# RWKV recurrence in chunks of 64 on four 64x64 array tiles, its output transposed and packed by DMA

## The chip, the cores and the metric

The kernel runs on one core of a Trainium2 chip. A core has a matrix engine (TensorE; PE in the profile, its weight loads PEld), three elementwise engines (VectorE, ScalarE, GpSimd; DVE, ACT, POOL) and a queue engine (SyncE, SP) that here issues every DMA. Each engine works through its own instruction list in order and waits on semaphores for the others. The metric is the device time of one execution, in microseconds (us), as the median of several runs.

## The reference

A recurrence (RWKV-6) over 4 batches, 8 heads, 768 time steps and 48 channels per head, followed by a two-layer MLP on the result, 3072 tokens of 384 channels:

```
for t in range(S):                       # per batch and head
    cur   = outer(u * k_t, v_t)          # [48, 48]
    y_t   = r_t @ (state + cur)
    state = w_t[:, None] * state + outer(k_t, v_t)
x = y.transpose(0, 2, 1, 3).reshape(3072, 384)
h = x @ w_in                             # [384, 2048]
out = gelu_exact(h) @ w_out              # [2048, 384]
```

The two weight matrices arrive as float64 and are turned into float32 on the chip.

## The kernel before

**The recurrence.** Two heads side by side fill the 128 partitions, 64 each (48 channels and zeros). The 768 steps of a head pair are 6 chunks of 128. Inside a chunk every pair (s, t) with s < t belongs to one of seven levels, h = 1 to 64. At each level one matrix product per chunk (`d`, line 191) gives all products of k (stationary, 128 columns) with the right halves of r (moving, 64 steps for each of two heads), and a masked copy out of PSUM (line 196, VectorE; for the last level a plain copy on ScalarE, line 194) keeps those of the level in `a`. Then r and k are multiplied by the other half's decay (line 205 on VectorE, a call for each head's 64 partitions; line 206 on GpSimd), and the halves' products `tots` are formed (line 208). The next level's `d` needs both. The diagonal (s = t) is a product apart: r times k on GpSimd (line 171), a matrix product with u (`dg_ps`, line 175), and `dv` on GpSimd (line 180). r lies in blocks with zeros for the other head, which is why one k serves both heads.

After the levels: transposes of k (`kt_ps`, line 218), each chunk's k v^T (`kv_ps`, line 223, the only products on part of the array: two 64-column halves), the states in front of the chunks one after the other (line 229, VectorE), and y (lines 236 and 238: `a` or r is stationary with 128 columns, v or the state moves with 48). y is in time-major order, so line 252 transposes x on TensorE into `xT` for the MLP.

**The MLP.** For 384 tokens at a time: 16 blocks of 3 products `h_ps` (line 262) and a GELU on ScalarE (line 265), then 3 blocks of 16 products `o_ps` (line 271), a copy (line 276) and the output's DMA.

**The order of the work.** Python generators set it. `attention` yields after each level; two head pairs go side by side, and after each yield some steps of the MLP of the batch before are put in. A scheduler then places the instructions on the engines by its own estimates. For the first batch the steps put in are instead the conversion of the weights: 28 pieces, each with a DMA, one ScalarE, five VectorE (lines 132 to 141) and one GpSimd instruction. The MLP of batch 0 therefore begins with the recurrence of batch 1, and the MLP of the last batch stands alone at the end. PSUM's 8 banks: 2 for `d`, 3 for the MLP, 2 for `misc`, 1 for y.

All data are float32. Each float32 product of the program is two weight loads and two matrix instructions in the trace (transposes are one), so the counts of the trace are twice the program's.

Of the kernel before, what the change touches and what calls it, by code (L numbers as in the profile page):

```python
# [20 lines left out]
DC = 3           # chunks of which a PSUM bank takes a level's products  # L21
PIECE = 512      # float64s of a row converted at once
# [7 lines left out]
def kernel(  # L30
    ctx: ExitStack,
    tc: tile.TileContext,
    rkw: bass.AP,      # [batch * head pair, 128, 3, time]: r, k, w, channels on partitions
    v: bass.AP,        # [batch * head pair, 128, 2, chunk, channel]: time on partitions
    u: bass.AP,        # [128, head pair, 2]: a head's u in its rows and its column, zeros elsewhere
# [15 lines left out]
    NU, _, _, S = rkw.shape  # L51
    D = v.shape[-1]
    NP = u.shape[1]
    B = NU // NP
    NC = S // C
    HC = C // 2
    N_TOK, DM = out.shape
    NJ = DM // 128
    DF = w_in.shape[1]
    NF = DF // 128  # L60
    TB = S // 2
    NT = TB // 128
# [9 lines left out]
    # r of a pair's heads in blocks, [head, channel] x [head, time]: zeros in the other two.  # L72
    r_bufs = [const.tile([128, 2, S], F32, name=f"r{i}") for i in range(4)]
    for r in r_bufs:
        nc.gpsimd.memset(r[0:G, 1, :], 0.0)
        nc.gpsimd.memset(r[G:, 0, :], 0.0)

    loaded = {}

    def load(n):  # L80
        if n >= NU:
            return
        r = r_bufs[n % len(r_bufs)]
        for g in range(2):
            nc.sync.dma_start(out=r[g * G:(g + 1) * G, g, :], in_=rkw[n, g * G:(g + 1) * G, 0, :])
        kw = io.tile([128, 2, S], F32, name="kw_in")
        nc.sync.dma_start(out=kw, in_=rkw[n, :, 1:3, :])
        x = io.tile([128, 2, NC, D], F32, name="v_in")
        nc.sync.dma_start(out=x, in_=v[n])
        loaded[n] = r, kw, x  # L90

    load(0)
    load(1)
    u_sb = const.tile([128, NP, 2], F32, name="u_sb")
    nc.sync.dma_start(out=u_sb, in_=u)

# [3 lines left out]
    # masks[h][s, (q, j)]: whether s is in the left half of the block q of 2h steps.  # L100
    masks = {}
    for h in LEVELS[:-1]:
        m = wk.tile([128, HC], F32, name="maskf")
        mv = m.rearrange("p (q j) -> p q j", j=h)
        nc.gpsimd.memset(m, 1.0)
        nc.gpsimd.affine_select(out=mv, in_=mv, compare_op=ALU.is_ge, fill=0.0, base=0,
                                pattern=[[-2 * h, HC // h], [0, h]], channel_multiplier=1)
        nc.gpsimd.affine_select(out=mv, in_=mv, compare_op=ALU.is_ge, fill=0.0, base=h - 1,
                                pattern=[[2 * h, HC // h], [0, h]], channel_multiplier=-1)
        masks[h] = const.tile([128, 1, HC], U8, name=f"mask{h}")  # L110
# [3 lines left out]
    a_bufs = [const.tile([128, NC, 2, C], F32, name=f"a{i}") for i in range(2)]  # L114
    for a in a_bufs:
        nc.vector.memset(a, 0.0)
# [4 lines left out]
    def to_float32(dst, src):  # L121
        """dst = src, float64s of which src's int64s hold the bits, rounded to float32."""
        n = src.shape[1]
        raw = cv.tile([128, PIECE], I64, name="raw")[:, 0:n]
# [5 lines left out]
        # What float32 has no exponent for: to 0, or to the largest.  # L130
# [5 lines left out]
        # The sign, the exponent and the mantissa's first 20 bits.  # L136
        nc.vector.scalar_tensor_tensor(out=f, in0=hi, scalar=0xC0000000, in1=f,  # L137
                                       op0=ALU.bitwise_and, op1=ALU.bitwise_or)
        # The other 32, as a number below the 20th; the sum rounds.
# [4 lines left out]

    def weights():
        pieces = [(w_in_sb[:, j, i:i + PIECE], w_in[j * 128:(j + 1) * 128, i:i + PIECE])
                  for i in range(0, DF, PIECE) for j in range(NJ)]
        pieces += [(w_out_sb[:, f, :], w_out[f * 128:(f + 1) * 128, :]) for f in range(NF)]
        for dst, src in pieces:
            if wide:  # L150
# [7 lines left out]
    def attention(n):  # L158
# [5 lines left out]
        if b not in x_of:  # L164
            x_of[b] = wk.tile([128, NC, DM], F32, name="x", bufs=1)
# [176 lines left out]
```

## Time and profile before

| | |
|---|---|
| median of 3 runs | 967.09 us (963.03 to 967.88) |
| profiled execution, span | 961.1 us |
| PE busy, weight loads busy | 860.9 us (90%), 623.9 us (65%) |
| VectorE, GpSimd, ScalarE busy | 447.7, 243.3, 123.3 us |
| instructions in the profile | 10766, of which 4248 matrix instructions |
| DMA | 41.59 MB, mean 43 GB/s |

The profiled execution's own time is its span, 961.1 us; the runs' median is 6 us above it. A row of the groups reads: line, engine, operation, tiles written and read, shape, count, then busy time and the mean length of one instruction. Mean lengths of matrix instructions contain the pipeline's depth, so the distance between starts says more: a merged row of the timeline or of the chain gives a count and the time they took together. PEclk is the share of TensorE's clock that was granted in a stage.

### The profile page before, as it was taken

To read this page: it belongs to the slowest core of one execution; us is meant where nothing else is said; L and a number is where in the kernel's file an instruction comes from. 1 tells how busy PE (TensorE), PEld (TensorE's weight loads), DVE (VectorE), ACT (ScalarE), POOL (GpSimd) and SP (SyncE) were. 2 spreads that over 40 slices of the span, in tenths; PEclk is the share of its full clock that TensorE was granted. 3 is DMA by queue.
4 is the path that set the end of the run, shared out by engine and by line. 5 is a ranking of instruction groups with operands and counts; after the bars stand their busy time and mean duration, and the time that the engine had idled before them with its cause. 6 is when DMAs were issued, how large, how long until landed. Compare 5 with 4: busy or idle time off the path is not lost.

```text
span 961.1 us, 10766 instructions
## 1 busy us (share of the span) xinstructions
PE 860.9 (90%) x4248; PEld 623.9 (65%) x4248; DVE 447.7 (47%) x812; ACT 123.3 (13%) x262; POOL 243.3 (25%) x236
## 2 busy tenths in 40 slices
PE   3748654889998999989998999989998999999998
PEld 3638653766766776766766676857676766655554
DVE  6898799875542553245533554155333543000000
ACT  0012010221110111011100111111100111120110
POOL 8645634334102411052204220052103210000000
PEclk9876556679999999989998999989998999999999
DMA  9033322420022001200031002200000000000000
GB/s 286 5 109 140 110 82 83 131 75 1 1 83 67 1 0 45 96 8 1 1 98 51 1 1 83 66 1 1 9 9 9 1 1 17 9 0 17 9 0 25
DMA packets 14850, 41.59 MB, mean 43 GB/s; under 512 B 2000, under 2 KB 5072, under 8 KB 14800
## 3 DMA queue, kind: packets, MB, share of 16 engines
q1 hardware_dynamic: 14800, 40.91, 13.2%
q8 instruction: 34, 0.56, 0.2%
q14 instruction: 16, 0.13, 0.0%
HBM read 36.18 MB, written 4.72 MB: 43 GB/s over the span
## 4 chain that ended last, share of the span: by engine, by line
PE 60%; issue 24%; DVE 11%; POOL 4%; DMA 1%; SPq 0%; ACT 0%; POOLq 0%
PE h_ps L262 26%; PE o_ps L271 14%; PE d L191 13%; DVE r L205 3%; DVE a L196 2%; PE dg_ps L175 2%; PE y L236 2%; POOL rk L171 2%; PE y L238 2%; DVE f L137 1%; DVE f L132 1%; DVE e L141 1%; DVE e L140 1%; DMA r<-in_rkw_dram 1%; POOL kw_in L206 1%
## 5 line engine op out<-in xcount | busy, mean ns | idle before, releaser
L262 PE MATMUL h_ps<-xT,w_in_sb 128*128 128x384 f32 x768 | 269.6, 503 | 0.0
L191 PE MATMUL d<-r,kw_in 128*128 128x128 f32 (+1 forms) x1344 | 207.9, 311 | 64.1 <-DVE a L196 54.6
L271 PE MATMUL o_ps<-w_out_sb,gt 128*128 128x384 f32 x768 | 260.8, 490 | 0.0
L191 PEld LDWEIGHTS d<-r,kw_in 128*128 128x128 f32 (+1 forms) x1344 | 193.0, 212 | 92.7 <-issue 49.7
L262 PEld LDWEIGHTS h_ps<-xT,w_in_sb 128*128 128x128 f32 x768 | 146.9, 198 | 90.7 <-issue 10.1
L196 DVE COPY_PREDICATED a<-mask,d 128x384 f32<-128x384 uint8 x192 | 131.8, 724 | 156.4 <-PE d L191 152.3
L271 PEld LDWEIGHTS o_ps<-w_out_sb,gt 128*128 128x128 f32 x768 | 141.2, 190 | 87.2 <-issue 1.0
L206 POOL TENSOR_TENSOR kw_in<-kw_in,tots 128x384 f32<-128x384 f32 x96 | 92.7, 966 | 289.7 <-PE d L191 281.1
L205 DVE TENSOR_TENSOR r<-r,tots 64x384 f32<-64x384 f32 x192 | 128.8, 671 | 44.0 <-PE d L191 40.9
L171 POOL TENSOR_TENSOR rk<-r,kw_in 64x768 f32<-64x768 f32 x32 | 60.3, 1885 | 203.3 <-PE dg_ps L175 201.2
L265 ACT ACTIVATE gt<-h_ps 128x384 f32<-128x384 f32 x128 | 62.7, 490 | 295.8 <-PE h_ps L262 295.8
L276 DVE COPY o_sb<-o_ps 128x384 f32<-128x384 f32 x24 | 13.4, 558 | 163.7 <-PE o_ps L271 163.7
L236 PE MATMUL y<-v_in,a 128*128 128x48 f32 x384 | 77.1, 300 | 1.1 <-DVE x L241 1.1
L236 PEld LDWEIGHTS y<-v_in,a 128*128 128x128 f32 x384 | 63.9, 216 | 12.1 <-DVE x L241 9.8
L238 PE MATMUL y<-state,r 128*128 128x48 f32 x320 | 68.0, 297 | 1.0 <-DVE state L229 0.6
L175 PE MATMUL dg_ps<-u_sb,rk 128*128 128x2 f32 x192 | 31.6, 292 | 28.0 <-POOL rk L171 24.6
L238 PEld LDWEIGHTS y<-state,r 128*128 128x128 f32 x320 | 54.6, 214 | 1.6 <-DVE state L229 1.0
L241 DVE TENSOR_TENSOR x<-y,dv 128x288 f32<-128x288 f32 x32 | 14.6, 457 | 86.8 <-PE y L238 86.8
L175 PEld LDWEIGHTS dg_ps<-u_sb,rk 128*128 128x128 f32 x192 | 31.3, 250 | 32.4 <-POOL rk L171 27.8
L205 DVE TENSOR_TENSOR r<-r,kw_in 64x384 f32<-64x384 f32 x32 | 39.5, 1233 | 2.4 <-POOL rk L171 1.9
L131 ACT ACTIVATE f<-raw 128x384 f32<-128x384 f32 (+1 forms) x28 | 16.9, 605 | 121.2 <-DMA raw<-in_w_out_dram 65.5
L208 DVE TENSOR_TENSOR tots<-tots 128x192 f32<-128x192 f32 (+5 forms) x96 | 30.4, 323 | 1.4
(37 smaller groups left out, 325.5 us busy)
## 6 DMA issues: line engine op xcount, KB each, us to landing
kw_in<-in_rkw_dram SPq DMA_DIRECT2D x16, 768.0 KB, 4.3
r<-in_rkw_dram SPq DMA_DIRECT2D x32, 192.0 KB, 3.2
raw<-in_w_in_dram SPq DMA_DIRECT2D x12, 512.0 KB, 3.6
raw<-in_w_out_dram SPq DMA_DIRECT2D x16, 384.0 KB, 3.0
v_in<-in_v_dram SPq DMA_DIRECT2D x16, 288.0 KB, 3.5
out_dram<-o_sb SPq DMA_DIRECT2D x24, 192.0 KB, 1.9
u_sb<-in_u_dram SPq DMA_DIRECT2D x1, 4.0 KB, 9.6
```

Source lines behind the costliest of these rows:

```text
L171: nc.gpsimd.tensor_mul(rk[half[g]], r[half[g], g], k[half[g]])
L175: nc.tensor.matmul(dg_ps[:, c, :], lhsT=rk[:, c * C:(c + 1) * C], rhs=u_sb[:, p, :], start=True, stop=True)
L191: nc.tensor.matmul(d[0:m, c - c0], lhsT=k[:, c * C:c * C + m], rhs=right[:, :, c], start=True, stop=True)
L196: nc.vector.copy_predicated(out=to[:, c0:c0 + DC].rearrange("p c g q j -> p (c g) q j"), mask=masks[h].rearrange("p o (q j) -> p o q j", j ...
L205: nc.vector.tensor_mul(r2, r2, t2[half[g], :, 0:1].to_broadcast([G, nb, h]))
L206: nc.gpsimd.tensor_mul(k2, k2, t2[:, :, 1:2].to_broadcast([128, nb, h]))
L208: nc.vector.tensor_mul(new, t2[:, :, 0], t2[:, :, 1])
L236: nc.tensor.matmul(y[:, c, :], lhsT=at[:, c, g, :], rhs=vt[:, g, c, :], start=True, stop=(c == 0))
L238: nc.tensor.matmul(y[:, c, :], lhsT=r[:, g, c * C:(c + 1) * C], rhs=state[:, c - 1, :], start=False, stop=True)
L262: nc.tensor.matmul(h_ps, lhsT=w_in_sb[:, j, f * 128:(f + 1) * 128], rhs=xT[:, j, :], start=(j == 0), stop=(j == NJ - 1))
L265: nc.scalar.activation(out=gt, in_=h_ps, func=AF.Gelu)
L271: nc.tensor.matmul(o_ps, lhsT=gs[f][:, i * 128:(i + 1) * 128], rhs=w_out_sb[:, f, :], start=(f == 0), stop=(f == NF - 1))
```

## The change

The chunks are 64 steps long instead of 128, so that k (64 partitions of a head, 64 steps) and `a` (64 by 64) fit a quarter of the array. There are now six levels, h = 1 to 32, and the work goes in tiles of 384 tokens: a tile has all 8 heads in two units of four heads (two head pairs, on the free axis). Eight tiles, 16 units.

- `products` (line 194) makes 24 products of 64x64 per level and unit; partition half g of the operands and half p of the output choose one of four array tiles, and the loop visits all four in turn. r is no longer laid out in blocks with zeros.
- The diagonal becomes a seventh set of such products, of k with r times u (`ru`, ScalarE, line 190), masked by the identity (line 204). `rk`, `dg` and `dv` are gone.
- Line 227 multiplies r for both heads in one call of 128 partitions.
- kv and y are 64x64 products too. y is computed transposed (v or the state stationary, `a` or r moving; lines 268 and 284), with all of a unit in two PSUM banks; the state's products wait for the first y products through a small VectorE copy (`fence`). States carry from one tile to the next of a batch.
- ScalarE copies y to `ysb`, and DMAs on SP's queue (line 295) put each head's 48 rows at its place in `xT`, in 10 pieces per tile. TensorE's transposes of x are gone.
- The main loop: during tile x's recurrence the MLP of tile x - 1 is put in, a step or more after each yield. The w_in pieces are converted in tile 0, the w_out pieces in tile 1 beside the MLP of tile 0. The four last steps or so of an MLP come after the recurrence's last yield.
- PSUM: 3 buffers of 2 banks for everything of the recurrence, 2 banks for the MLP.

How the instructions of TensorE stand in the middle of a batch, a level of two head pairs (r_73, r_74) and the next, before:

```order
L262 MATMUL h_ps<-xT,w_in_sb 128x384 x8
L191 MATMUL d<-r_73,kw_in 128x128 x6
L262 MATMUL h_ps<-xT,w_in_sb 128x384
L191 MATMUL d<-r_74,kw_in 128x128 x6
L262 MATMUL h_ps<-xT,w_in_sb 128x384 x8
```

And in the change, the diagonal and the first levels of a tile, both units (24 products each) in one row:

```order
L199 MATMUL d<-ru,rkw_in 64x64 x48
L311 MATMUL h_ps<-xT,w_in_sb 128x384 x9
L199 MATMUL d<-rkw_in 64x32 x48
L311 MATMUL h_ps<-xT,w_in_sb 128x384 x6
L199 MATMUL d<-rkw_in 64x32 x48
```

A level is now 48 small products instead of 12 large ones, with 6 products of the MLP behind it (9 before).

The end of a pair's recurrence and the beginning of the next on TensorE, before (v, a and the state make y; rk is GpSimd's r times k):

```order
L238 MATMUL y<-state,r_74 128x48
L271 MATMUL o_ps<-w_out_sb,gt 128x384 x9
L175 MATMUL dg_ps<-u_sb,rk 128x2 x6
L191 MATMUL d<-r_75,kw_in 128x128 x6
L262 MATMUL h_ps<-xT,w_in_sb 128x384
```

The same place in the change (st_147 and st_145 hold states):

```order
L284 MATMUL y_ps<-rkw_in,st_147 64x64
L284 MATMUL y_ps<-rkw_in,st_145 64x64 x8
L320 MATMUL o_ps<-w_out_sb,gt 128x384 x24
L199 MATMUL d<-ru,rkw_in 64x64 x48
L311 MATMUL h_ps<-xT,w_in_sb 128x384 x9
```

The 24 products of the MLP's end stand between the last y products of a tile and the first `h_ps` of the next, which read the packed `xT`.

VectorE in tile 1 of the change, where the conversion of w_out (lines 148 to 157) shares it with the levels (a_140 and a_141 are the two units' `a`):

```order
L220 COPY_PREDICATED a_140<-mask_122,d 128x48x8
L153 SCALAR_TENSOR_TENSOR f<-raw,f 128x384
L227 TENSOR_TENSOR rkw_in<-rkw_in,tots 128x48x8
L156 TENSOR_SCALAR e<-f 128x384
L148 TENSOR_SCALAR f<-f 128x384
L157 SCALAR_TENSOR_TENSOR e<-raw,e 128x384
L150 TENSOR_SCALAR f<-f 128x384
L220 COPY_PREDICATED a_141<-mask_122,d 128x48x8
```

In before all 28 pieces stood so among the levels of the first batch, with no product of the MLP beside them.

The diff, cut to its core:

```diff
-C = 128          # time steps of a chunk
-LEVELS = (1, 2, 4, 8, 16, 32, 64)
+C = 64
+T = 384
+Q = 2
+NC = T // C
+N3 = NC // 2
+NI = Q * N3
+LEVELS = (1, 2, 4, 8, 16, 32)
+BANK = 512
...
-    def attention(n):
+    def attention(n):
+        x, un = divmod(n, UB)
+        first = x % HALVES == 0
...
+        ru = wk.tile([128, Q * T], F32, name="ru")
+        for q in range(Q):
+            nc.scalar.activation(out=ru[:, q * T:(q + 1) * T], in_=r[:, q * T:(q + 1) * T], func=AF.Copy,
+                                 scale=u_sb[:, un * Q + q:un * Q + q + 1])
+        ruc = ru.rearrange("p (i c t) -> p i c t", c=2, t=C)
+
+        def products(right, width):
+            d = ps.tile([128, 2, BANK], F32, name="d", tag="d", bufs=3)
+            for i in range(NI):
+                for g in range(2):
+                    for p in range(2):
+                        nc.tensor.matmul(d[half[p], g, i * width:(i + 1) * width],
+                                         lhsT=kc[half[g], i, p], rhs=right(half[g], i, p), start=True, stop=True)
+            return d[:, :, 0:NI * width]
+
+        d = products(lambda z, i, p: ruc[z, i, p], C)
+        nc.vector.copy_predicated(out=at.rearrange("p g i t -> p (g i) t"),
+                                  mask=masks[0].to_broadcast([128, 2 * NI, C]), data=d)
+        yield
...
-            for g in range(2):
-                r2 = r[half[g], g].rearrange("p (n two j) -> p n two j", two=2, j=h)[:, :, 1, :]
-                nc.vector.tensor_mul(r2, r2, t2[half[g], :, 0:1].to_broadcast([G, nb, h]))
+            nc.vector.tensor_mul(r2, r2, t2[:, :, 0:1].to_broadcast([128, nb, h]))
...
+        for i in range(NI):
+            for p in range(2):
+                for g in range(2):
+                    nc.tensor.matmul(kv_ps[half[g], p, i * D:(i + 1) * D], lhsT=kt[half[p], i, g, :],
+                                     rhs=vc[i][g][half[p], 0:D], start=True, stop=True)
...
+        y_ps = ps.tile([128, 2, BANK], F32, name="y_ps", tag="d", bufs=3)
+        for i in range(NI):
+            for p in range(2):
+                for g in range(2):
+                    nc.tensor.matmul(y_ps[half[g], p, i * C:(i + 1) * C], lhsT=vc[i][g][half[p]],
+                                     rhs=at[half[p], g, i, :], start=(i == 0), stop=True, skip_group_check=True)
+        fence = wk.tile([128, 2], F32, name="fence")
+        nc.vector.tensor_copy(out=fence, in_=y_ps[:, :, NI * C - 1])
+        yield
+        for i in range(NI):
+            q, c3 = divmod(i, N3)
+            for p in range(2):
+                for g in range(2):
+                    c = 2 * c3 + (p + g) % 2
+                    src, c0 = (st, c - 1) if c else (before, NC - 1)
+                    if src is None:
+                        continue
+                    o = (q * NC + c0) * D
+                    nc.tensor.matmul(y_ps[half[g], c % 2, i * C:(i + 1) * C], lhsT=src[half[g], o:o + G],
+                                     rhs=rc[half[g], i, c % 2], start=False, stop=True, skip_group_check=True)
+        ysb = wk.tile([128, Q * T], F32, name="ysb")
+        nc.scalar.copy(out=ysb.rearrange("p (i c t) -> p c i t", c=2, t=C),
+                       in_=y_ps[:, :, 0:NI * C].rearrange("p c (i t) -> p c i t", t=C))
+        for q in range(Q):
+            for g in range(2):
...
+                    nc.sync.dma_start(out=xT[f0 % 128:f0 % 128 + f1 - f0, f0 // 128, :],
+                                      in_=ysb[e:e + f1 - f0, q * T:(q + 1) * T])
...
+        load(n + 2 * UB)
+        yield
...
+    for x in range(NX):
+        slots = zip(*(attention(x * UB + i) for i in range(UB)))
+        if x == 0:
+            spread(slots, weights(in_pieces), len(in_pieces), len(in_pieces))
+        else:
+            steps = mlp(x - 1)
+            if x == 1:
+                more = weights(out_pieces)
+                def both(a=steps, b=more):
+                    for _ in a:
+                        next(b, None)
+                        yield
+                steps = both()
+            n = NF + NT * NF // 4
+            spread(slots, steps, n, n - 4)
+    for _ in mlp(NX - 1):
+        pass
```

More of the change, by code (lines that the diff above doesn't have):

```diff
@@ L70 @@
     ps = ctx.enter_context(tc.tile_pool(name="ps", bufs=1, space=PSUM))
[L73 to L76, printed above, removed]
+    half = [slice(0, 64), slice(64, 128)]
     loaded = {}
@@ L123, in to_float32 @@
         n = src.shape[1]
[L124 removed]
+        raw = cv.tile([128, PIECE], I64, name="raw", bufs=3)[:, 0:n]
         nc.sync.dma_start(out=raw, in_=src)
@@ L143, in to_float32, with weights @@
         nc.gpsimd.tensor_add(dst, f.bitcast(F32), e.bitcast(F32))
[L145 to L148, printed above, removed]
+    def weights(pieces):
         for dst, src in pieces:
@@ L283 @@
[L283 to L295 removed]
+        kt_ps = ps.tile([128, 2, BANK], F32, name="kt_ps", tag="d", bufs=3)
```

288 lines of the change are left out of this document (139 added, 149 removed).

## The prediction

> **What bounds the kernel now.** I first cut the span into stages: the first batch's recurrence, three batches of recurrence with the MLP of the batch before, and the last MLP (busy time by engine, with the number of instructions).
>
> ```profile
> 0.00:212.00 212.00, 134.10 (x726) 122.08 (x726) 178.93 (x318) 29.98 (x58) 109.28 (x110) 0.72 0.36 116
> 212.00:420.00 208.00, 200.37 (x1061) 143.54 (x1061) 96.07 (x179) 25.63 (x57) 50.46 (x47) 0.98 0.11 35
> 420.00:628.00 208.00, 203.13 (x1055) 144.46 (x1055) 87.74 (x163) 26.11 (x58) 44.16 (x43) 0.97 0.11 35
> 628.00:836.00 208.00, 201.75 (x1032) 142.59 (x1033) 81.59 (x149) 26.17 (x58) 39.44 (x39) 0.97 0.02 7
> 836.00:961.10 125.10, 121.55 (x377) 71.25 (x375) 3.35 (x6) 15.37 (x32) 0.00 (x0) 1.00 0.03 10
> ```
>
> In the first stage VectorE is busy 179 of 212 us, and PE, at 0.72 of its clock, only 134: that stage belongs to VectorE. In the next three PE is busy 200 to 203 of 208 us: they belong to PE, and VectorE has half its time free. So I price the steady stages on PE and the start on VectorE. How far apart matrix instructions start stands in the chain of waits (two rows) and in the timeline of PE (two rows).
>
> ```profile
> 224.78 5.16 PE h_ps L262 x16
> 229.94 1.34 PE d L191 x12
> ...
> 500.61 0.39 PE L238 MATMUL y<-state,r 128*128 128x48 f32 x2
> 500.83 0.39 PE L236 MATMUL y<-v_in,a 128*128 128x48 f32 x2
> ```
>
> An MLP instruction takes 5.16 / 16 = 322 ns, one of `d` 1.34 / 12 = 112 ns, and one of y (0.83 - 0.61) / 2 = 0.11 us although it moves only 48 columns. What y and `d` share is the load of 128 weight columns, so the load sets the pace of all small products. The groups give the counts:
>
> ```profile
> L262 PE MATMUL h_ps<-xT,w_in_sb 128*128 128x384 f32 x768 | 269.6, 503 | 0.0
> L191 PE MATMUL d<-r,kw_in 128*128 128x128 f32 (+1 forms) x1344 | 207.9, 311 | 64.1 <-DVE a L196 54.6 <-DMA kw_in<-in_rkw_dram 9.5
> L271 PE MATMUL o_ps<-w_out_sb,gt 128*128 128x384 f32 x768 | 260.8, 490 | 0.0
> L236 PE MATMUL y<-v_in,a 128*128 128x48 f32 x384 | 77.1, 300 | 1.1 <-DVE x L241 1.1
> L238 PE MATMUL y<-state,r 128*128 128x48 f32 x320 | 68.0, 297 | 1.0 <-DVE state L229 0.6 <-DVE state L227 0.3
> L175 PE MATMUL dg_ps<-u_sb,rk 128*128 128x2 f32 x192 | 31.6, 292 | 28.0 <-POOL rk L171 24.6
> ```
>
> Per batch that is 384 MLP instructions (124 us) and 336 + 176 + 48 of the recurrence (560 x 0.112 = 63 us), with some 6 us for transposes and kv: 193 of the stage's 208. The rest is idle time and clock, part of it at each pair's beginning, where `dg_ps` waits for GpSimd:
>
> ```profile
> 418.94 2.01 PE L175 MATMUL dg_ps<-u_sb,rk 128*128 128x2 f32 x12 [4.06 <-POOL rk L171]
> ```
>
> **The price of a small product.** Per tile of 384 tokens the change issues, in trace instructions, 2 units x 7 sets x 24 x 2 = 672 for the levels and the diagonal, 96 for kv, 96 for the first part of y and 96 for the states' part: 960 on 64x64 tiles, where before had 560 / 2 = 280 large ones and 40 of kv. Everything depends on what one costs. The one group of before on part of the array is kv (two column halves); beside it the 64-column `d` of the last level, all on one half. The timeline, weight loads in 60 ns windows from each group's start (kv, then `d`), and the whole kv group with its neighbours:
>
> ```profile
> 806.08 0.14 PEld L223 LDWEIGHTS kv_ps<-v_in,kt 128*64 128x64 f32 x2 [0.38 <-issue]
> ...
> 368.06 0.13 PEld L191 LDWEIGHTS d<-r,kw_in 128*64 128x64 f32 x1 [0.55 <-issue]
> ...
> 805.88 0.27 PE L218 MATMUL kt_ps<-ident,kw_in 128*128 128x128 f32 x1
> 806.08 0.66 PEld L223 LDWEIGHTS kv_ps<-v_in,kt 128*64 128x64 f32 x20 [0.38 <-issue]
> 806.09 0.79 PE L223 MATMUL kv_ps<-v_in,kt 128*64 128x48 f32 x20
> 806.80 1.56 PE L271 MATMUL o_ps<-w_out_sb,gt 128*128 128x384 f32 x4
> ```
>
> The 20 kv loads start over 0.66 - 0.14 = 0.52 us, 27 ns apart, and with the odd gap 29. In the first 60 ns two loads start where the two halves alternate and one where all is on one half. In the program the two instructions of one product follow each other on the same half, so the second start must be the other half's product, taken past a waiting one. One half thus starts a load about every 58 ns, half of y's 112 for half the columns, and the two halves run independently. **Bounds for the change:** 58 / 4 = 14.5 ns if four tiles run as these two do; 29 if no more than two starts fit into 58 ns; 58 if tiles in different rows don't overlap at all. I take 14.5: kv is the nearest row, and its second load passing a blocked one is what four tiles need. The states' products use only two of the four tiles (g decides both halves), so 29 there. What kv can't show is a long stream: its 40 instructions may have been queued behind 322-ns products, while a set here has 96 loads.
>
> [...]
>
> Changing between shapes costs too: from kt's start to kv's 0.21 us where 0.11 is normal, and from the last kv start (806.08 + 0.52) to the MLP's 0.20. I take 0.2 us per group, there and back, 11 groups per tile: 2.2 us.
>
> **A steady tile.** MLP 192 x 0.322 = 61.9; small products 864 x 0.0145 + 96 x 0.029 = 15.3; 12 transposes of k at 0.11 = 1.3; changes of shape 2.2; 1.5 for stalls and clock. Sum 82.2 us, against 104 now.
>
> Does anything else bind? VectorE, from its groups and POOL's:
>
> ```profile
> L196 DVE COPY_PREDICATED a<-mask,d 128x384 f32<-128x384 uint8 x192 | 131.8, 724 | 156.4 <-PE d L191 152.3
> L205 DVE TENSOR_TENSOR r<-r,tots 64x384 f32<-64x384 f32 x192 | 128.8, 671 | 44.0 <-PE d L191 40.9
> L205 DVE TENSOR_TENSOR r<-r,kw_in 64x384 f32<-64x384 f32 x32 | 39.5, 1233 | 2.4 <-POOL rk L171 1.9
> L208 DVE TENSOR_TENSOR tots<-tots 128x192 f32<-128x192 f32 (+5 forms) x96 | 30.4, 323 | 1.4
> L206 POOL TENSOR_TENSOR kw_in<-kw_in,tots 128x384 f32<-128x384 f32 x96 | 92.7, 966 | 289.7 <-PE d L191 281.1
> L229 DVE SCALAR_TENSOR_TENSOR state<-state,tots,kv_ps 128x48 f32<-128x48 f32 x64 | 16.2, 261 | 1.0
> ```
>
> A unit needs a 768-wide masked copy (two 384-wide ones as bound: 1.45), five of 0.72, r 1.23 + 5 x 0.67 (one call for both heads: half of before's calls), `tots` about 2.2, states 11 x 0.26 and the fence: 15 us, 30 per tile of 82. Within a level both units need 2 x (0.72 + 0.67) = 2.8 us of VectorE and 2 x 0.97 of POOL before the next set may start; behind the set stand 6 MLP products, 12 x 0.322 = 3.9 us. Covered, with 1 us to spare. The states, 2 x 2.9 us in a row, and behind them on VectorE the fences, have 8 MLP products (5.2 us), y's first part and 8 more. Without that cover a level would show up to 2.8 us, 17 us per tile. The diagonal's 24 products per unit are in the 960; rk, `dg` and `dv`, and the 4-us wait above, are gone.
>
> The pack: 10 DMAs per tile on SP wait for ScalarE's copy, behind them the next loads and outputs, none needed soon. A DMA lands in 2 to 4 us here:
>
> ```profile
> kw_in<-in_rkw_dram SPq DMA_DIRECT2D x16, 768.0 KB, 4.3
> out_dram<-o_sb SPq DMA_DIRECT2D x24, 192.0 KB, 1.9
> ```
>
> 24 MLP products (48 x 0.322 = 15.5 us) and the next diagonal stand between the last y and the first use of `xT`: nothing on the path; without them some 5 us per tile.
>
> **The start.** VectorE also converts the weights:
>
> ```profile
> L137 DVE SCALAR_TENSOR_TENSOR f<-raw,f 128x384 uint32<-128x384 uint32 (+1 forms) x28 | 18.6, 664 | 0.3
> L141 DVE SCALAR_TENSOR_TENSOR e<-raw,e 128x384 f32<-128x384 uint32 (+1 forms) x28 | 18.5, 660 | 0.1
> L140 DVE TENSOR_SCALAR e<-f 128x384 uint32<-128x384 uint32 (+1 forms) x28 | 18.0, 644 | 0.1
> L132 DVE TENSOR_SCALAR f<-f 128x384 f32<-128x384 f32 (+1 forms) x28 | 17.7, 634 | 0.9 <-ACT f L131 0.7
> L134 DVE TENSOR_SCALAR f<-f 128x384 uint32<-128x384 uint32 (+1 forms) x28 | 15.1, 541 | 0.2
> ...
> 16.67 1.15 POOL kw_in L206
> ```
>
> That is 88 us, unchanged, beside 30 for tile 0 and 24 for tile 1's levels. Loaded data are first worked on at 16.7 us. With VectorE busy 95% of the time from there (179 of about 189 us now): 17 + 142 / 0.95 = 166. Then tile 1 has its 96 `o_ps` instructions left, 31 us, and kv, y and the shapes, 8; 5 more for PE's half clock among VectorE's waits. Tile 1's recurrence ends at 210 us. Before, the recurrence of two tiles ended at 212 with no MLP done; now one tile's MLP, 62 us, is done as well.
>
> **The sum.** 210 + 6 x 82.2 + the last MLP 61.9 + its end 3.6 = 769 us of span. The end is from the last rows:
>
> ```profile
> 954.81 2.74 PE L271 MATMUL o_ps<-w_out_sb,gt 128*128 128x384 f32 x8
> 957.59 0.56 DVE L276 COPY o_sb<-o_ps 128x384 f32<-128x384 f32 x1 [9.76 <-PE o_ps L271]
> ```
>
> The profiled span of 961 lies 6 us under the median of the runs, so the median is 775.
>
> **Rivals.** *Two at a time:* no more than two starts per 58 ns, by order of issue or by a floor on starts. A tile is 61.9 + 960 x 0.029 + 1.3 + 2.2 + 1.5 = 94.7, the start some 6 more: 216 + 568 + 65.5 + 6 = 856. For it: in program order the same tile's two instructions follow each other, and no stream closer than 27 ns is in the trace. Against it: the two loads in 60 ns. [...] *Not faster but slower:* row tiles don't overlap, or a long stream of loads can't be supplied faster than one per 58 ns. A tile is 61.9 + 55.7 + 5.0 = 122.6, tile 1 is then PE's too: 222 + 736 + 65.5 + 6 = 1029. It decides from 48 ns per instruction, where the sum reaches 967. For it: y's 112 ns per pair of load and product is the fastest long stream in the trace. Against it: that pace is explained by 128 columns. *The clock falls:* if short groups don't hold the granted clock, a third of the MLP at half speed adds 20 us per tile: about 900. Against it: 0.97 in stages where PE is busy 97%.
>
> **How the numbers follow.** Four tiles at once 0.54, two at a time 0.34, no overlap 0.08, the clock 0.04. The likeliest gives 775, alone 740 to 800 (the start 15 us either way, 3 us per tile). The range takes in the second case: 738 to 868. About 0.5% can be told from no change here; faster takes the first two and most of the clock: 0.90, same 0.02, slower 0.08.
>
> **What would show it.** Weight loads of `d` 14 to 15 ns apart in a set, 96 in about 1.4 us; steady tiles of about 82 us with PE busy throughout; VectorE busy up to some 165 us; first `h_ps` of a tile without a wait for DMA. A set of 2.8 us means the second case, 5.6 us the third. A wait of `d` for VectorE in steady tiles would break the cover.

## The result and the profile after

| | before | after |
|---|---|---|
| median | 965.06 us (963.01 to 967.88) | 741.70 us (740.78 to 742.57) |
| ratio | | 0.7684, 95% interval 0.7658 to 0.7711 |
| span of the profiled execution | 961.1 us | 740.9 us |
| PE, VectorE, GpSimd, ScalarE busy | 860.9, 447.7, 243.3, 123.3 us | 679.4, 284.6, 151.6, 137.9 us |
| matrix instructions | 4248 | 9296 |

The change is faster by 23%. The forecast was 775 us, in a range of 738 to 868: right in kind, 33 us too long, and the measured time lies only 4 us inside the lower end of the range.

The stages of after, in the view by windows (start and end, length, busy time and count of PE, PEld, DVE, ACT, POOL, then the granted clock, DMA share, GB/s):

```profile
33.00:84.00 51.00, 22.68 (x619) 19.64 (x612) 50.85 (x99) 12.18 (x19) 21.57 (x17) 0.70 0.48 149
84.00:143.50 59.50, 46.90 (x584) 29.16 (x584) 50.17 (x96) 18.90 (x38) 28.29 (x25) 0.89 0.35 116
143.50:183.50 40.00, 39.52 (x388) 24.51 (x388) 13.78 (x49) 4.34 (x7) 3.15 (x3) 0.96 0.33 107
183.50:265.50 82.00, 82.00 (x1169) 53.21 (x1168) 25.47 (x63) 14.95 (x28) 13.27 (x12) 1.00 0.16 52
...
675.60:740.90 65.30, 61.89 (x192) 36.10 (x190) 2.23 (x4) 7.84 (x16) 0.00 (x0) 1.00 0.03 12
```

Read from the bottom: the last MLP alone, 65.3 us, and a steady tile (the next one is as long) of 82.0 us in which PE is busy throughout at full clock and VectorE for 25 us. Up to 143.5 us VectorE is the bound (50.85 of 51 us in the first row, with PE at 0.70 of its clock, and 50.17 of 59.5 in the second). Then 40 us belong to PE. The sum is 183.5 + 6 x 82.0 + 65.3 = 741.

The 220 us between the two spans divide so: the six steady tiles took 82 instead of 104 us each (132 us); at the end one tile's MLP is left instead of two (125.1 - 65.3 = 60 us); and the first 183.5 us hold two tiles' recurrence and one MLP, where before 212 us held the recurrence alone (28 us). Of the 22 us per steady tile some 16 are PE's work for the recurrence (34 us before, 31 for the large products and 3 for transposes and kv; 18.1 now), and the rest is idle time and clock that the 208 us of before still held. The 60 us at the end come from working in tiles of 384 tokens. No run has that order with the large products, so what it would give by itself is not shown.

A steady tile in the chain of waits of after (start, length, what):

```profile
183.54 1.56 PE d L199 x96
...
191.10 1.53 PE d L199 x96
192.63 4.07 PE h_ps L311 x12
...
226.63 1.31 PE kt_ps L238 x12
...
233.10 1.54 PE kv_ps L248 x96
...
240.01 1.56 PE y_ps L268 x96
...
246.92 2.94 PE y_ps L284 x96
249.87 15.68 PE o_ps L320 x48
265.55 1.56 PE d L199 x96
```

Every piece is PE's: no wait for VectorE, GpSimd or a DMA stands in it. A set of 96 takes 1.53 us, 16 ns per instruction with the change of shape in it. The states' products (L284), which use two tiles at a time, take 2.94 us, or 31 ns each. How densely the starts lie shows the timeline of PEld in the first 50 ns and in the first 90 ns of a set:

```profile
191.03 0.15 PEld L199 LDWEIGHTS d<-rkw_in 64*64 64x64 f32 x4 [0.55 <-issue]
...
191.03 0.21 PEld L199 LDWEIGHTS d<-rkw_in 64*64 64x64 f32 x8 [0.55 <-issue]
```

Four loads start 6 to 7 ns apart, none for the next 35 ns, and then four again: each array tile starts one load about every 58 ns, and the four run side by side. Before, two started in 60 ns. The groups show that the pack's DMAs are hidden: of the 2.0 us that all `h_ps` waited for them nothing lies in the tile above.

```profile
L311 PE MATMUL h_ps<-xT,w_in_sb 128*128 128x384 f32 x768 | 266.0, 499 | 2.0 <-DMA xT<-ysb 2.0
...
xT<-ysb SPq DMA_DIRECT2D x48, 72.0 KB, 3.2
```

### The profile page after: what moved, and what is told of

Its sections match the earlier page's. It is cut to its first block, busy times and chain, and to the rows that moved or that the text cites. A ratio compares the mean times of both kernels' runs of the same rounds, so it can differ in the third digit from the quotient of the medians.

```text
span 740.9 us, 20544 instructions
## 1 busy us (share of the span) xinstructions
PE 679.4 (92%) x9296; PEld 444.6 (60%) x9296; DVE 284.6 (38%) x644; ACT 137.9 (19%) x254; POOL 151.6 (20%) x166
## 4 chain that ended last, share of the span: by engine, by line
PE 84%; DVE 10%; DMA 3%; issue 2%; POOL 1%; ACT 0%; SPq 0%; POOLq 0%; DVEq 0%
PE o_ps L320 34%; PE h_ps L311 33%; PE d L199 10%; PE y_ps L284 3%; DVE rkw_in L227 2%; DVE f L153 2%; DMA v_in<-in_v_dram 2%; PE y_ps L268 1%; PE kv_ps L248 1%; DVE f L148 1%; DVE e L156 1%; DVE e L157 1%; PE kt_ps L238 1%; DVE f L150 1%; DMA rkw_in<-in_rkw_dram 1%
## 5 line engine op out<-in xcount | busy, mean ns | idle before, releaser
L311 PEld LDWEIGHTS h_ps<-xT,w_in_sb 128*128 128x128 f32 x768 | 143.5, 192 | 94.8 <-issue 3.0
L228 POOL TENSOR_TENSOR rkw_in<-rkw_in,tots 128x384 f32<-128x384 f32 x80 | 83.7, 1063 | 135.2 <-PE d L199 131.6
L199 PEld LDWEIGHTS d<-rkw_in 64*64 64x64 f32 x4608 | 82.2, 148 | 46.0 <-issue 26.4
L199 PE MATMUL d<-rkw_in 64*64 64x32 f32 x4608 | 88.3, 231 | 20.2 <-DVE rkw_in L227 19.7
L220 DVE COPY_PREDICATED a<-mask,d 128x384 f32<-128x384 uint8 x80 | 59.9, 749 | 102.0 <-PE d L199 101.7
L228 POOL TENSOR_TENSOR rkw_in<-rkw_in 128x384 f32<-128x384 f32 x16 | 21.0, 1333 | 294.6 <-PE d L199 294.6
L227 DVE TENSOR_TENSOR rkw_in<-rkw_in,tots 128x384 f32<-128x384 f32 x80 | 67.3, 841 | 31.1 <-PE d L199 30.2
L259 DVE SCALAR_TENSOR_TENSOR st<-st,tots,kv_ps 128x48 f32<-128x48 f32 x160 | 30.0, 259 | 33.3 <-PE kv_ps L248 33.2
L284 PEld LDWEIGHTS y_ps<-rkw_in,st 64*64 64x64 f32 x752 | 24.5, 144 | 4.1 <-issue 3.8
L153 DVE SCALAR_TENSOR_TENSOR f<-raw,f 128x384 uint32<-128x384 uint32 (+1 forms) x28 | 26.1, 931 | 0.2
L284 PE MATMUL y_ps<-rkw_in,st 64*64 64x64 f32 x752 | 25.6, 229 | 0.1
```

The costliest lines, as they stand in the source:

```text
L199: nc.tensor.matmul(d[half[p], g, i * width:(i + 1) * width], lhsT=kc[half[g], i, p], rhs=right(half[g], i, p), start=True, stop=True)
L220: nc.vector.copy_predicated(out=to, mask=masks[h].rearrange("p o (q j) -> p o q j", j=h).to_broadcast([128, 2 * NI, m, h]), data=d)
L227: nc.vector.tensor_mul(r2, r2, t2[:, :, 0:1].to_broadcast([128, nb, h]))
L228: nc.gpsimd.tensor_mul(k2, k2, t2[:, :, 1:2].to_broadcast([128, nb, h]))
L259: nc.vector.scalar_tensor_tensor(out=stq[:, q, c], in0=stq[:, q, c - 1] if c else b4[:, q, NC - 1], scalar=totq[:, q, c:c + 1], in1=kvq[:, ...
L284: nc.tensor.matmul(y_ps[half[g], c % 2, i * C:(i + 1) * C], lhsT=src[half[g], o:o + G], rhs=rc[half[g], i, c % 2], start=False, stop=True, ...
```

## The experiments

Each is the changed kernel with one edit, the last two with a second one on top. Where no interval is given, the time is that of a single execution, and the reading rests on the trace.

### Four tiles in turn, or one after the other

Is it the four tiles that make a set short, and must the program visit them in turn? Three other orders of the loop in `products`, with the same 24 products per level and unit.

```diff
-            for i in range(NI):
-                for g in range(2):
-                    for p in range(2):
+            for g in range(2):
+                for p in range(2):
+                    for i in range(NI):
```

> The 24 products of a level and unit are issued tile by tile, six products (twelve weight loads) on one array tile before the next tile's. Same instructions, same results. Theory A (every array tile starts one load per 58 ns; the engine passes a waiting instruction only a few places ahead, so the order in the program decides): a set of 96 loads takes about 96 x 58 = 5.6 us in place of 1.53, a steady tile of tokens 82 + 7 x 4 = 110 us, the whole about 940 us. Rival B (the engine looks tens of instructions ahead and fills the tiles whatever the order): sets stay at 1.5 to 2.8 us, the whole 742 to 810 us. Rival C (the array tiles matter little, the gain is from the removed waits and the shorter list of work): below 770 us.

It took 917.03 us. Its chain of waits among the levels of a steady tile:

```profile
458.74 4.26 PE d L199 x96
463.01 5.76 PE h_ps L311 x12
```

The window over that stretch:

```profile
448.70:473.00 24.30, 24.30 (x314) 18.61 (x313) 6.95 (x10) 2.46 (x5) 4.38 (x5) 0.86 0.01 1
```

And PEld in its timeline, from the first load of that set to 0.13 us after it:

```profile
458.67 0.25 PEld L199 LDWEIGHTS d<-rkw_in 64*64 64x64 f32 x3 [0.55 <-issue]
```

A set takes 4.26 us instead of 1.53, 44 ns per instruction. Within a tile the loads start 55 to 59 ns apart (the three of the row are the first), and 96 of them would need 5.6 us. A set has seven places where the tile changes; the 1.3 us that are missing are 0.19 us at each, three or four starts. The starts in the trace agree: at a change of tile eight loads in a row stand 25 to 33 ns apart, as four of the old tile and four of the next in turn would. So, as these starts are read, PE does pass a waiting product, but here by only about three or four starts at each change: the order of the program has to bring the tiles close together. (The trace has the starts and not the instruction list; that the list follows the loop is taken for granted here.)

The second part had not been expected: the twelve MLP instructions behind the set took 5.76 us instead of 4.07, and the mean clock of the window is 0.86, although PE is recorded as busy for all of the 24.3 us. The clock fell to half for 3.4 us right behind a stretch that a set had nearly filled:

```profile
449.72:453.13 3.41, 3.41 (x79) 3.37 (x78) 1.53 (x3) 0.00 (x0) 0.92 (x2) 1.00 0.00 0
453.13:456.54 3.41, 3.41 (x6) 1.77 (x6) 1.31 (x2) 0.00 (x0) 0.89 (x1) 0.50 0.00 0
```

Seven sets x 2.73 = 19 us, and the 5 to 8.5 us lost in three to five stretches of 3.4 us at half clock per tile, make tiles of 106 to 109.5 us.

The other two orders use two tiles at a time, in the two column halves (g outside, then i and p inside), and in the two row halves (p outside, then i and g):

```diff
-            for i in range(NI):
-                for g in range(2):
+            for g in range(2):
+                for i in range(NI):
                     for p in range(2):
```

> Products of one half of the rows first, alternating between the two column halves, then those of the other half. Theory A: two tiles at a time, 29 ns per load, 2.8 us per set, a steady tile 82 + 7 x 1.3 = 91 us, the whole about 808 us. Rival B (look-ahead of tens of instructions): 742 to 755 us, since the other row half's products are at most 24 loads away.

```diff
-            for i in range(NI):
-                for g in range(2):
-                    for p in range(2):
+            for p in range(2):
+                for i in range(NI):
+                    for g in range(2):
```

> Products of one column half first, alternating between the two row halves, which write different PSUM banks of the same partitions. Theory A: as with two columns, 2.8 us per set and about 808 us. Rival (row halves below one another share the path to PSUM and don't overlap; in the change only the columns did, and something else hides it): 5.6 us per set, about 940 us.

They took 780.33 and 778.11 us. In the chains of waits, columns first:

```profile
458.95 2.32 PE d L199 x96
461.27 4.07 PE h_ps L311 x12
```

And rows:

```profile
456.76 2.32 PE d L199 x96
```

Both are 24 ns per instruction, where 29 had been expected: 96 x 29 = 2.8 us less what passes at the places where the pair changes. Tiles became 7 x 0.79 = 5.5 us longer (87.6 us), and the MLP kept its 4.07 us. Row halves overlap just as column halves do. That rules out the third case of the prediction, rows that don't overlap, by a set of its own, and it settles the order of sizes: 55 to 59 ns from load to load on one tile, 24 (31 for the states) per instruction on two, 16 on four.

### Without the cover of the pack

The four last steps of an MLP are put in before the recurrence's last yield, so that nothing stands between the last y and the next `h_ps` but the diagonal.

```diff
-    N_SLOTS = len(LEVELS) + 5
+    N_SLOTS = len(LEVELS) + 4
...
-            spread(slots, steps, n, n - 4)
+            spread(slots, steps, n, n)
```

> All of an MLP's steps are put between the yields of the recurrence, so no MLP products stand between a tile's last y and the next tile's first use of xT; only the diagonal and the first level (3 us) do. The prediction's price for the pack without cover is some 5 us per tile, less these 3 us: PE idle for 2 to 5 us at each of 7 turns, the whole 756 to 777 us. Rival (the DMA's 3.2 us are within the two sets): 742 to 746 us.

It took 786.59 us, 45 more than the change. Its chain of waits at the seam of two tiles:

```profile
443.95 1.57 PE y_ps L284 x48
...
447.72 6.96 DMA xT<-ysb
...
454.72 2.93 PE h_ps L311 x4
```

The windows of the tile before (from diagonal to diagonal) and of the 91.8 us that hold this seam (from transposes to transposes):

```profile
357.92:446.62 88.70, 85.72 (x1171) 55.17 (x1170) 25.39 (x63) 14.95 (x28) 12.72 (x12) 0.96 0.15 48
418.50:510.30 91.80, 87.01 (x1167) 55.76 (x1165) 25.40 (x63) 14.94 (x28) 13.01 (x12) 0.94 0.15 47
```

From the last y to the first `h_ps` 9.2 us pass: ScalarE's copy (0.81 us), SP's issues, and a DMA of 6.96 us. The diagonal and the first level fill half of it. Then four `h_ps` take 2.93 us, 0.73 each instead of 0.32, as at half clock (0.79 each for two of them in the next run at a granted clock of 0.50); the mean clock of the 91.8 us is 0.94. This seam is one of the two worst. The other steady tiles took 88.7 to 89.2 us, 6.7 to 7.2 more than in the change. In the first row PE is idle for 3.0 us, and in all steady tiles for 3.0 to 4.8, which is what was expected (2 to 5). What was not priced is the clock behind the wait: at 0.96 over the 88.7 us of the first row some 3.5 us of full clock are missing, by estimate some 7 us at half clock, and the tile's other 3.7 us of loss are put down to that. So the whole took longer than the 756 to 777 us expected.

### Without the cover of the levels

In steady tiles the MLP's products are left out between the levels and all put after the recurrence's last yield, except in tile 1.

```diff
-            spread(slots, steps, n, n - 4)
+            spread(slots, steps, n, n - 4 if x == 1 else 0)
```

> From tile 2 on no MLP step is put between the yields of the recurrence; nearly all of an MLP then stands in one piece between two tiles' recurrences (the scheduler still moves one h_ps product in front of each level). Theory of the prediction (VectorE and GpSimd of a level are hidden by the MLP's products, and show without them): up to 2.8 us per level and some 6 us for the states, PE idle for 12 to 25 us in a steady tile, which becomes 95 to 107 us plus what a halved clock costs; the whole 820 to 900 us. Rival (levels of two units side by side cover each other, so the order of the MLP matters little): steady tiles under 88 us, the whole under 780 us.

It took 797.29 us, less than expected and more than the rival. Here the scheduler still placed some products between the sets, so the cover shrank and did not vanish. The windows of two tiles and of a stretch of levels in the second:

```profile
365.09:452.73 87.64, 83.57 (x1166) 54.67 (x1165) 25.58 (x63) 14.95 (x28) 11.87 (x12) 1.00 0.15 49
452.73:546.37 93.64, 91.24 (x1165) 60.48 (x1164) 25.23 (x61) 14.95 (x28) 11.89 (x12) 0.89 0.14 46
460.00:470.00 10.00, 10.00 (x218) 7.12 (x210) 6.91 (x12) 0.49 (x1) 4.76 (x6) 0.50 0.01 3
```

PE in the timeline of the last stretch (a row's length reaches past the start of the next, 2.79 us against 2.72 in the first, so the starts are to be read):

```profile
461.96 2.79 PE L199 MATMUL d<-rkw_in 64*64 64x32 f32 x96
464.68 1.65 PE L311 MATMUL h_ps<-xT,w_in_sb 128*128 128x384 f32 x2
466.25 0.97 PE L199 MATMUL d<-rkw_in 64*64 64x32 f32 x28
```

The five tiles that can be told apart fall into two kinds. Two kept the full clock and took 87.6 and 87.8 us, 5.7 more than in the change, with PE idle for 4.1 to 4.7 of them: there the waits for the other engines show. Three took 93.6 to 95.3 us with PE idle for only 2.4 to 2.7: among their levels the granted clock is 0.50 for 20 to 24 us, PE is slower, and the waits vanish behind that. From start to start the set takes 2.72 us instead of 1.53, and the two MLP instructions 1.57, where 2 x 0.322 and 0.2 for the change of shape would be 0.84. So even what was taken of the cover is worth 5.7 us per tile at full clock and 12 to 13 where the clock falls, 10 on the average.

### The start: what VectorE does there

Four kernels change VectorE's work in the first two tiles. What each is worth is read at the transposes of tile 2 (`kt_ps`, 226.63 us in the change) and the next tile's (308.64).

First the calls of line 227 are cut in two, as before had them:

```diff
-            nc.vector.tensor_mul(r2, r2, t2[:, :, 0:1].to_broadcast([128, nb, h]))
+            for z in half:
+                nc.vector.tensor_mul(r2[z], r2[z], t2[z, :, 0:1].to_broadcast([64, nb, h]))
```

> The multiplication of r at each level is two VectorE calls of 64 partitions again, as before the change, in place of one of 128. It adds 6 x 2 calls of some 0.7 us per tile of tokens, 8 us. Theory (VectorE sets the end of the first two tiles' recurrence and has cover in the steady tiles): about 16 us of VectorE more up to tile 1's last level, of which 10 to 14 show, steady tiles stay within 1 us of 82.0; the whole 752 to 760 us. Rival (a level has no room left: 2 x (0.75 + 1.4) = 4.3 us of VectorE behind 4.07 us of MLP products): steady tiles 83 to 86 us, the whole 765 to 780 us. Rival (the start is not VectorE's): 742 to 745 us.

749.71 us (748.56 to 751.01; ratio to before 0.7775, 0.7749 to 0.7780). Its chain of waits:

```profile
232.97 1.31 PE kt_ps L239 x12
...
314.98 1.31 PE kt_ps L239 x12
```

Six more us in the start, fewer than the 10 to 14 expected, and then 82.0 per tile as in the change: in steady tiles twelve more calls of VectorE cost nothing, as the cover has it; in the start they are paid.

Next the program has the w_out pieces too in tile 0, ahead of any MLP:

```diff
-            spread(slots, weights(in_pieces), len(in_pieces), len(in_pieces))
+            spread(slots, weights(in_pieces + out_pieces), len(in_pieces) + len(out_pieces), len(in_pieces) + len(out_pieces))
...
-            if x == 1:
+            if x < 0:
```

> All 28 weight pieces are converted in tile 0, as the kernel before did in its first batch; tile 1 then has the MLP of tile 0 beside it and no conversion. Theory (VectorE's conversion of w_out runs under TensorE's work in tile 1 only if it stands there): tile 0 gets some 40 us longer, tile 1 becomes a steady tile of 82 us instead of about 100; the whole 760 to 768 us. Rival (VectorE's total before steady state sets the end whatever the order): 741 to 746 us.

752.58 us (751.14 to 753.26; 0.7802, 0.7776 to 0.7827). Its chain of waits has the transposes of tile 2 at

```profile
237.22 1.31 PE kt_ps L238 x12
```

and a window of the start reads

```profile
50.00:80.00 30.00, 1.56 (x48) 1.40 (x48) 29.93 (x63) 5.86 (x9) 11.63 (x9) 0.50 0.49 155
```

VectorE is full from 50 to 80 us (29.93 of 30) while PE does 1.56 us of work. All in all 10.6 us are lost, between the two expectations. The edit did less than was meant, as VectorE's groups from the first `h_ps` on (90.87 us; 78.90 in the change) show:

```profile
L153 DVE SCALAR_TENSOR_TENSOR f<-raw,f 128x384 uint32<-128x384 uint32 x12 | 7.5, 628 | 0.1
```

Twelve of the 28 pieces were still converted beside the first MLP, where in the change it was seventeen: the scheduler let five more go ahead of the MLP, and not all. So part of the start's gain is that tile 0's MLP runs beside the conversion; what all of it is worth was not measured.

Then the conversion loses an instruction. The low word is shifted and or-ed in, which cuts the mantissa where it was rounded, instead of being scaled on VectorE in two instructions and added on GpSimd:

```diff
-        e = cv.tile([128, PIECE], U32, name="e")[:, 0:n]
...
-        nc.vector.tensor_scalar(out=e, in0=f, scalar1=0xFF800000, scalar2=None, op0=ALU.bitwise_and)
-        nc.vector.scalar_tensor_tensor(out=e.bitcast(F32), in0=lo, scalar=2.0 ** -52, in1=e.bitcast(F32),
-                                       op0=ALU.mult, op1=ALU.mult)
-        nc.gpsimd.tensor_add(dst, f.bitcast(F32), e.bitcast(F32))
+        nc.vector.scalar_tensor_tensor(out=dst.bitcast(U32), in0=lo, scalar=29, in1=f,
+                                       op0=ALU.logical_shift_right, op1=ALU.bitwise_or)
```

> The conversion of a weight piece ends with one VectorE instruction that puts the low word's top three bits under the 20 mantissa bits (float32 by cutting off instead of rounding), in place of two VectorE instructions and a GpSimd addition. It takes 28 x (0.49 + 0.65 - 0.65) = 14 us from VectorE and 36 us from GpSimd ahead of tile 1's last level. Theory (VectorE's work sets the end of the start): 10 to 18 us less, the whole 724 to 732 us. Rival (the chain of levels between TensorE, VectorE and GpSimd sets it): 738 to 742 us.

721.76 us (720.25 to 724.28; 0.7487, 0.7458 to 0.7516), 20 less than the change and below the 724 to 732 expected. Its chain of waits:

```profile
204.31 1.31 PE kt_ps L235 x12
286.32 1.31 PE kt_ps L235 x12
```

VectorE's groups up to 125 us:

```profile
L152 DVE SCALAR_TENSOR_TENSOR f<-raw,f 128x384 uint32<-128x384 uint32 (+1 forms) x28 | 18.7, 669 | 0.3
...
L224 DVE TENSOR_TENSOR rkw_in<-rkw_in,tots 128x384 f32<-128x384 f32 x20 | 13.6, 678 | 0.0
```

All of the gain lies in the start (22 us), as the theory had it. It is more than the instruction that was saved: the two shown became shorter as well. In the change's groups up to 143.5 us the saved one and these two read

```profile
L153 DVE SCALAR_TENSOR_TENSOR f<-raw,f 128x384 uint32<-128x384 uint32 (+1 forms) x26 | 23.6, 906 | 0.1
L227 DVE TENSOR_TENSOR rkw_in<-rkw_in,tots 128x384 f32<-128x384 f32 x20 | 20.1, 1007 | 0.0
...
L156 DVE TENSOR_SCALAR e<-f 128x384 uint32<-128x384 uint32 (+1 forms) x25 | 12.3, 494 | 0.1
```

12.3 us were saved outright; the other two are 237 and 329 ns shorter per call now that GpSimd's additions are gone. Whether these had lengthened them stays open: before had the same additions, and there the first of the two (line 137) took 664 ns, and in the run with the calls cut in two, which has them as well, it took 694.

On top of that the clip (line 148) goes to GpSimd, whose addition is gone:

```diff
-        nc.vector.tensor_scalar(out=f.bitcast(F32), in0=f.bitcast(F32), scalar1=as_float(0x38000000),
+        nc.gpsimd.tensor_scalar(out=f.bitcast(F32), in0=f.bitcast(F32), scalar1=as_float(0x38000000),
```

> As v1, and the clipping to float32's range goes to GpSimd: 28 x 0.5 = 14 us less of VectorE again, some 28 x 0.8 = 22 us of GpSimd. Theory: another 5 to 12 us less than v1, the whole 715 to 726 us. Rival (GpSimd slows VectorE while both work, or the chain through a third engine delays pieces): no faster than v1, 726 to 740 us.

737.60 us (736.14 to 738.67; 0.765, 0.7619 to 0.768): the rival was right. The groups of GpSimd and of VectorE, from 20 to 140 us:

```profile
L147 POOL TENSOR_SCALAR f<-f 128x384 f32<-128x384 f32 (+1 forms) x28 | 53.2, 1902 | 29.2 <-ACT f L146 28.7 <-PE d L196 0.6
...
L149 DVE TENSOR_SCALAR f<-f 128x384 uint32<-128x384 uint32 (+1 forms) x27 | 16.6, 615 | 26.6 <-POOL f L147 26.3
```

A clip takes GpSimd 1.9 us, where 0.8 had been expected and VectorE takes 0.5, and VectorE now waits 26 us for it.

Last, the shorter conversion with more buffers, since VectorE waits for loads and for ScalarE in it (between 20 and 140 us its chain holds five of w_in's and w_out's DMAs, 20.8 us in all):

```diff
-        raw = cv.tile([128, PIECE], I64, name="raw", bufs=3)[:, 0:n]
+        raw = cv.tile([128, PIECE], I64, name="raw", bufs=6)[:, 0:n]
...
-        f = cv.tile([128, PIECE], U32, name="f")[:, 0:n]
+        f = cv.tile([128, PIECE], U32, name="f", bufs=3)[:, 0:n]
```

> As v1, with six buffers instead of three for the float64 pieces and three instead of two for the piece in work, in the room that the dropped buffer leaves, so that a piece's DMA is issued earlier. In v1 ScalarE and VectorE waited for these DMAs between 45 and 66 us and again at 102 and 117 us, some 20 us in all. Theory (those waits are on the path until TensorE is full): 6 to 14 us less than v1, the whole 708 to 716 us. Rival (other waits of the levels take their place): within 3 us of v1, 719 to 725 us.

718.76 us (718.28 to 718.90; 0.7456, 0.7425 to 0.7487), the lowest median of all. It lies 3 us below the version without the buffers, and the two profiled spans (717.2 and 718.5 us) are 1.3 us apart; the intervals of the ratios overlap, so no gain is shown; the rival (within 3 us) comes closest. A window of the start, first of the kernel without the buffers:

```profile
50.00:80.00 30.00, 14.04 (x383) 12.09 (x384) 25.86 (x67) 8.99 (x13) 2.59 (x3) 0.64 0.64 205
```

And with them:

```profile
50.00:80.00 30.00, 17.60 (x356) 13.19 (x357) 27.88 (x78) 9.04 (x14) 2.33 (x2) 0.66 0.73 250
```

VectorE gains 2 us of work in 30 there; of the 6 to 14 us expected hardly any reaches the end.

## Why the prediction was right, and where it was long

Span by span, forecast against measured:

| step | forecast | after |
|---|---|---|
| VectorE's stage of the start ends | 166 | 143.5 |
| the rest of tile 1 on PE (31 + 8) | 39 | 40.0 |
| 5 us for half clock in the start | 5 | 0 |
| a steady tile | 82.2 | 82.0 |
| last MLP and its end | 65.5 | 65.3 |
| median less span | 6 | 0.8 |

**Price of a small product.** Taken at 14.5 ns from the kv starts, with 29 for two tiles. Measured 1.53 us per set, of which 1.39 is 96 x 14.5, and 2.94 for the states' 96, of which 2.78 is 96 x 29. The lowest of the three bounds was right, for the reason given: each tile starts a load about every 58 ns with the others at work, and every 55 to 59 ns alone. At two tiles and at one tile the runs gave 24 and 44 ns, less than 29 and 58 by what passes where the tile changes. "Two at a time" would need sets of 2.8 us and "no overlap" 5.6; neither is there. The long stream that kv couldn't show is in the trace of after: on different tiles four loads start in 50 ns, eight in 90, and 96 take 1.53 us.

**A steady tile.** Small products with their changes of shape and the transposes took 18.1 us (seven sets 10.7, kt 1.3, kv 1.5, y 1.6, states 2.9); the MLP's groups 63.9, 0.2 us above 12 x 0.322 for each group, or 2 in all. Together 82.0. The 1.5 us set aside for stalls were not needed, while the changes of shape took 3.5 instead of 2.2. These two offset each other, so that the sum came out within 0.2 us is partly luck.

**The covers.** No `d` waits in a steady tile, and no `h_ps` either; both covers hold. What they are worth was mis-sized. With the levels' cover thinned out a tile lost 5.7 us, and 12 to 13 where the clock fell (17 of waits had been the most); the pack's cover is worth 6.7 us or more per turn, of which 3.0 to 4.8 are waits and the rest is clock, instead of 5.

**The start, where 26.5 of the 33 us are lost.** The mis-sized term is "17 + 142 / 0.95 = 166". 142 was a sum of instructions' lengths; the 95% a share made of busy time, in which time is counted once. The two don't fit together, since one VectorE instruction's record reaches into the next one's. The 95% was misread as well: the 179 us contain 8 from ahead of the first loaded data, and from there to the stage's end before has 170.90 of 195.30, a share of 0.875, which by itself would have made the forecast still longer:

```profile
16.70:212.00 195.30, 130.23 (x711) 118.44 (x710) 170.90 (x303) 28.70 (x57) 96.14 (x86) 0.69 0.32 103
```

The timeline of after shows how records overlap:

```profile
56.86 0.41 DVE L156 TENSOR_SCALAR e<-f 128x512 uint32<-128x512 uint32 x1
57.19 0.42 DVE L148 TENSOR_SCALAR f<-f 128x512 f32<-128x512 f32 x1
```

The first begins at 56.86 and is 0.41 long, but the second begins at 57.19, 0.08 us before the end. In the whole stage:

```profile
0.00:143.50 143.50, 85.92 (x1736) 64.38 (x1736) 119.49 (x232) 38.20 (x68) 69.17 (x91) 0.85 0.45 154
17.00:143.50 126.50, 80.29 (x1544) 59.07 (x1544) 114.83 (x219) 33.55 (x61) 60.27 (x60) 0.82 0.39 129
```

The groups' lengths of these 232 instructions add up to 137 us, busy are 119.5, 0.872 of it. (The same could have been seen before: 198 us of lengths in the first 212 us, against 178.9 busy.) The step from 17 us on was put at 149.5 us and took 126.5: lengths of 137 instead of 142 make 5 us, the overlap 18, work done ahead of 17 us another 5, and a share of 114.83 / 126.5 = 0.91 instead of 0.95 takes 5 to 6 back. The 137 us are close to 142 by offsets: 77 of conversion instead of 88, since only 25 or 26 of the 28 pieces lie in the stage, 57 of the recurrence instead of 54, with line 227 at 1007 ns a call instead of 671, and 3 for masks. The other 5 us, for PE's half clock, were charged again although `o_ps` ran at 0.96 of the clock by then.

**The offset of the median.** Taking over the 6 us between span and median cost 5 more. A run's time is not its span but lies 1.6 to 2.0 us above it in every run listed; the rest of the 6 us was that the profiled execution of before was among its shortest (its span makes some 963 us). That of after, 742.57 us, was its longest, which left 0.8.

**The rivals.** "The clock falls" did not come about in the change, which has 1.00 in its steady tiles. But it is real: three of the runs above show it in steady tiles with the same products in another order (0.86 over 24.3 us with one tile at a time, 0.94 over 91.8 us without the cover of the pack, 0.50 over 10 us without that of the levels). It was held off by the argument that PE is busy; that argument is not enough, as PE is recorded busy for all of the 24.3 and of the 10 us.

## What to carry to other kernels

Where the trace shows that weight loads set the pace of small products (in before 0.11 us for 128 weight columns, whether 48 or 128 columns move), cut them to a part of the array and let the program visit the parts in turn, one product each: here 16 ns. The same products tile by tile took 44, and lost most of the gain (917 us, against 742 for the change and 961 before). Put products that fill the array between the sets: here they hid the other engines' work, with the clock at 1.00 in steady tiles; with that cover thinned out a tile took 5.7 to 13 us more. Before adding up an engine's instructions, compare the sum of their lengths with its busy time in a stage where it is full, and scale by that.

## What was not expected of the hardware

- Half clock with a busy PE. In 460 to 470 us of the run without products between the levels PE is recorded busy for 10.00 of 10 us, and the granted clock is 0.50; with one tile at a time the mean was 0.86 over 24.3 us of recorded busy PE. Sets on two tiles (2.32 us) or four (1.53) between 4.07 us of MLP left it at 1.00. So it does not follow the recorded busy time alone. In the run without products between the levels the three low stretches began behind waits of PE of 1.4 to 1.7 us (1.43 and 0.26 ahead of the one shown), but the tile from 365.09 us kept 1.00 with PE idle for 4.07 us, and the low state then held for 20 to 24 us of busy PE. What the clock follows was not shown.
- The reach of passing, as the starts are read, is small: in kv of before one product on another tile starts ahead of one that waits (two loads in 60 ns), and the 4.26 us of the run tile by tile leave room for only about three or four starts at each change of tile.
- Row halves of the array ran as independently as column halves: 2.32 us per set both ways.
- The landing of a packing DMA is not one number. In the last two tiles of the change, where no load of the next inputs goes ahead of them, the ten land in a median of 2.1 us; in the five tiles before, where a load of 1152 KB is issued less than 1 us ahead, the median is 3.2 to 5.0 and the longest 7.0. That the load is the reason was not tested by a run.
